# One row block of w3 loaded as float32 through ScalarE's DMA queue and cast on VectorE, in a fused recurrence and feed-forward kernel

## The chip, the cores and the metric

The kernel runs on one core of a Trainium2 chip. The metric is the device time of one execution in microseconds, lower being better. The engines are TensorE (PE; its weight loads are listed as PEld), VectorE (DVE), ScalarE (ACT), GpSimd (POOL) and SyncE (SP). They run side by side and wait for one another by semaphores. Each executes its own instructions strictly in the order in which the program lists them. DMAs are issued from the queues of SP, ACT and POOL.

## The reference

A gated linear recurrence over 768 steps, for 4 batches of 8 heads with 48 channels, gives `x` (3072 tokens by 384). A feed-forward block without a nonlinearity follows; its two elementwise factors are linear in `x`.

```
for t in range(S):
    cur = einsum('bhd,bhe->bhde', u[None] * kt, vt)
    y[:, :, t] = einsum('bhd,bhde->bhe', rt, state + cur)
    state = wt[:, :, :, None] * state + einsum('bhd,bhe->bhde', kt, vt)
a = x @ w1;  b = x @ w2          # 384 -> 1024
h = (a * b) @ w3                 # 1024 -> 1024
return h @ w_out                 # 1024 -> 384
```

Inputs and output are float32.

## The kernel before

**Weights.** Since `(a*b) @ w3 @ w_out = (a*b) @ (w3 @ w_out)`, the kernel first forms `w34 = w3 @ w_out` (1024 by 384). `w3` is kept as `w3_bf`, 8 row blocks of 128 rows by 1024 columns in bfloat16. For a row block `fi`, eight 128x128 pieces are transposed on PE into PSUM in two steps of four (`wt_fi_0` and `wt_fi_1`, columns 0 to 511 and 512 to 1023; L435). They are copied to SBUF in two steps (`w3Te_fi_h`, ACT or DVE, L443). Two steps of four matmuls against `wo_bf` follow (`wm_fi_0`, `wm_fi_1`, L449), and the sum is copied out as a block of `w34` (`w34e_fi`, L454).

**Recurrence.** The 768 positions are cut into 6 chunks of 128, and these into 13 units: the first two hold one batch each, the others two batches. A unit `t` loads `win`, `kin`, `rin`, `vin` (L401), takes a logarithm (`ln_t`, ACT), forms cumulative sums by a matmul against the triangular matrix `LT` (`cs_t`, L510, and for the first three units transposed, `csT_t`, L538), exponentials, products, transposes, masked scores (`m_t`, L671), outputs (`y_t`) and a state update (`kv_t`). In units 8 to 12 the transposes of r and k are DMA transposes on SP's queue (`dtr_t`, `dtk_t`, L593 and L608), and from unit 7 on that of y is too (`dty_t_b`, L733).

**Feed-forward.** A unit's output is multiplied by `w1` and `w2` (`a_t_g`, `b_t_g`, L797), the product is formed (`asb`, `abT`) and multiplied by `w34` (`o_t_b`, L821), copied (`osb`) and stored (`st`).

**Loads.** Everything that changes type on its way (r, k, v and all weights, float32 in memory, bfloat16 in SBUF) is issued by GpSimd, and so are the w tiles but the first. `w3` comes in six pieces: `w3_0` to `w3_3` are two row blocks by 512 columns each (`w3_1`: blocks 2 and 3, first half of the columns; `w3_3`: the same blocks, second half), `w3_4` is blocks 4 and 5 whole, `w3_5` blocks 6 and 7 whole. `w_out` comes in two halves, `wo_0` and `wo_1`. SP carries `win_0`, the row `u`, later the DMA transposes and the stores. Tiles are taken from small sets of buffers, so that a load may wait for an older reader of its buffer; a GpSimd load also waits for the landing of the eighth GpSimd load before it.

**What sets the order.** Two text tables do. `PLACES` says which buffer or PSUM bank each tile takes. `ORDER` lists every step with its engine; the program is emitted in exactly this order. A step named `warmB@N` issues N matmuls of zeros into bank B (L385). They compute nothing that is used, and they need only the `zeros` tile (L295). The constant `LT` is set to ones by DVE (step `ones`, L299) and made triangular by GpSimd (step `LT`, L310); `I128`, the identity for the transposes, is made in the same manner (steps `ones2` and `I128`, L314).

```
    def copier(eng):
        return nc.scalar.copy if eng == "ACT" else nc.vector.tensor_copy

    for n, (f0, f1, g0, g1) in enumerate(W3_PARTS):
        @op(f"w3_{n}")
        def _(eng, f=slice(f0, f1), gs=slice(g0, g1)):
            nc.gpsimd.dma_start(w3_bf[:, f, gs], w3r[:, f, gs])
```

Of the kernel before, what the change touches and what calls it, by code (L numbers as in the profile page):

```python
# [7 lines left out]
F32 = mybir.dt.float32  # L8
# [6 lines left out]
PAIRS = []  # L15
UNITS = [
# [35 lines left out]
W3_PARTS = [(0, 2, 0, 512), (2, 4, 0, 512), (0, 2, 512, 1024), (2, 4, 512, 1024), (4, 6, 0, 1024), (6, 8, 0, 1024)]  # L52
# [44 lines left out]
"""
ORDER = """
win_0@SP table@ACT padr_2@DVE padlw1@DVE ones2@DVE urow@SP w3_1@POOL padkk0@DVE padS1@DVE w3_5@POOL ones@DVE
padlw0@DVE padet0@DVE zeros@DVE win_1@POOL I128@POOL kin_0@POOL w3_3@POOL rin_0@POOL wo_0@POOL wo_1@POOL vin_0@POOL  # L100
warm6@17 wt_7_0@PE wt_7_1@PE w3_2@POOL wt_3_0@PE ln_1@ACT LT@POOL kin_1@POOL ln_0@ACT ucast@ACT rin_1@POOL warm6@8
wt_3_1@PE csT_1@PE w3_0@POOL cs_1@PE wt_2_0@PE rk_0@DVE ne_1@ACT wt_6_0@PE w3_4@POOL w3Te_7_0@DVE csT_0@PE
w3Te_3_0@ACT cs_0@PE padr_0@DVE padkk1@DVE umm@PE wt_6_1@PE wt_2_1@PE ucp@ACT ne_0@ACT ruk_0@DVE trr_0@PE w3Te_7_1@ACT
w3Te_3_1@DVE wm_7_0@PE win_2@POOL KRk_0@DVE w3Te_2_0@ACT padet1@DVE dg_0@DVE trk_0@PE pc_1@ACT wm_3_0@PE et_0@ACT
w3Te_6_0@DVE mask@POOL padS0@DVE trke_0@ACT wm_7_1@PE padr_1@DVE et_1@ACT vin_1@POOL KRr_0@DVE w3Te_6_1@DVE wm_3_1@PE
kin_2@POOL m_0_0@PE w34e_3@ACT wm_2_0@PE mcp_0_0@DVE pc_0@ACT rin_2@POOL wm_6_0@PE dv_0@DVE maff_0_0@DVE trr_1@PE
w1_1@POOL rk_1@DVE y_0@PE w34e_7@DVE yd_0@PE wm_6_1@PE win_3@POOL w3Te_2_1@DVE KRk_1@DVE wt_0_0@PE w34e_6@ACT
wt_1_0@PE yb_0@DVE wt_1_1@PE wm_2_1@PE w3Te_1_0@DVE KRr_1@DVE w3Te_1_1@ACT kv_0@PE padrr1@DVE wt_0_1@PE S_0@DVE
vin_2@POOL trk_1@PE w3Te_0_0@ACT wm_1_0@PE trke_1@DVE w34e_2@ACT ruk_1@DVE m_1_0@PE w3Te_0_1@DVE w1_0@POOL Sb_0@ACT
yt_0@PE mcp_1_0@DVE wm_1_1@PE wm_0_0@PE ln_2@ACT xT_0@DVE maff_1_0@DVE kin_3@POOL wm_0_1@PE dg_1@DVE w34e_1@ACT  # L110
dv_1@DVE cs_2@PE wt_4_0@PE rin_3@POOL padrr0@DVE ne_2@ACT y_1@PE yd_1@PE wt_4_1@PE csT_2@PE yb_1@ACT w3Te_4_0@DVE
wt_5_0@PE w2_0@POOL KRk_2@DVE pc_2@ACT wt_5_1@PE et_2@ACT w3Te_5_0@DVE trk_2@PE w3Te_4_1@DVE trr_2@PE w2_1@POOL
rk_2@DVE trke_2@ACT kv_1@PE KRr_2@DVE w1_3@POOL w3Te_5_1@ACT S_1@DVE warm1@2 m_2_1@PE ruk_2@DVE m_2_0@PE mcp_2_1@ACT
yt_1@PE mcp_2_0@DVE wm_4_0@PE ln_3@ACT wm_4_1@PE win_4@POOL maff_2_1@DVE maff_2_0@DVE wm_5_0@PE w34e_4@ACT dg_2@DVE
w34e_0@ACT y_2@PE w1_2@POOL iw_3@ACT cs_3@PE dv_2@DVE kv_2@PE ne_3@ACT vin_3@POOL a_0_0@PE S_2@DVE xT_1@ACT yd_2@PE
e_3@ACT KRk_3@DVE a_1_0@PE w2_2@POOL asb_0_0@DVE yb_2@ACT wm_5_1@PE pc_3@ACT rw_3@DVE yt_2@PE w34e_5@ACT rin_4@POOL
trk_3@PE asb_1_0@ACT KRr_3@DVE trke_3@ACT xT_2@DVE trr_3@PE w2_3@POOL rk_3@DVE b_2_0@PE trre_3@DVE a_2_0@PE kin_4@POOL
ruk_3@DVE m_3_0@PE asb_2_0@DVE m_3_1@PE win_5@POOL mcp_3_0@ACT a_2_1@PE abT_2_0@DVE b_0_0@PE mcp_3_1@ACT asb_2_1@DVE
b_1_0@PE abT_0_0@DVE Sb_1@ACT maff_3_1@POOL a_2_3@PE dg_3@DVE ln_4@ACT b_2_1@PE win_6@POOL Sb_2@ACT abT_1_0@DVE
# [54 lines left out]
def kernel(  # L174
# [248 lines left out]

    for n, (f0, f1, g0, g1) in enumerate(W3_PARTS):
        @op(f"w3_{n}")
        def _(eng, f=slice(f0, f1), gs=slice(g0, g1)):
            nc.gpsimd.dma_start(w3_bf[:, f, gs], w3r[:, f, gs])  # L427

    def w34_block(fi):
        for h in range(2):  # L430
            @op(f"wt_{fi}_{h}")
# [450 lines left out]
```

## Time and profile before

| | |
|---|---|
| three runs | 165.88, 169.48 and 171.12 us; median 169.48 us |
| the profiled execution | 166.03 us, of which the span from the first to the last instruction is 164.3 us |
| PE busy | 155.3 us, 94% of the span |
| DVE, ACT, POOL busy | 129.0, 111.0 and 77.4 us |
| DMA in GpSimd's queue | 16.06 MB |
| DMA in SP's queue | 8.72 MB |

The profile follows one execution. Its windows view gives the busy time of each engine in chosen stretches, its timeline the instructions in order of time (a row merges neighbours of one kind: start, duration from the first start to the last end, engine, line, operation, tiles, count, and in brackets the idle time before it with what ended it). The chain of waits goes back from the last instruction through whatever released each step. A DMA's time to landing runs from the start of its issue to the arrival of its completion semaphore. The names in rows are those of tiles; all weight tiles read as `w_bf` or `wo_bf`.

### The profile page before, as it was taken

The page shows a single profiled execution, that of the slowest core. Times are in us where ns is not written, and L with a number is a line of the kernel's source. Part 1 is how long each engine was busy: PE and PEld are TensorE (multiplying, and loading weights), DVE is VectorE, ACT ScalarE, POOL GpSimd, SP SyncE. Part 2 cuts the span into 40 slices and gives each one's busy share as a digit, 9 for nine tenths or more (in the row PEclk, how much of TensorE's full clock was granted, in tenths as well). Part 3 has the DMA queues.
Part 4 walks back from the last instruction along what each step waited for, and adds up shares of the span by engine and source line. Part 5 has one row for each costly group of instructions (what it writes and reads, how often), then busy time and mean ns, then how long its engine had stood idle before and what let it go on. Part 6 is the DMA issues. An engine that isn't in the chain of part 4 may idle for free.

```text
span 164.3 us, 4497 instructions
## 1 busy us (share of the span) xinstructions
PE 155.3 (94%) x1852; PEld 118.0 (72%) x1852; DVE 129.0 (79%) x229; ACT 111.0 (68%) x191; POOL 77.4 (47%) x80
## 2 busy tenths in 40 slices
PE   3979999999999999999999999979999999999991
PEld 1336566778897788877797976659779778888760
DVE  4004798999999999999999999969999998535440
ACT  3026637997998989999997889856989341325321
POOL 7956967787798878868379537000000000000000
PEclk9999999999999999999999999999999999999999
DMA  4999999999999999999999999999656230233132
GB/s 73 142 203 195 182 233 172 186 165 227 167 223 151 168 148 186 209 200 159 153 217 204 149 161 129 174 182 190 163 141 97 72 100 0 56 92 141 51 134 107
DMA packets 101606, 25.06 MB, mean 153 GB/s; under 512 B 91777, under 2 KB 99970, under 8 KB 101586
## 3 DMA queue, kind: packets, MB, share of 16 engines
q0 software_dynamic: 81536, 16.06, 116.0%
q1 hardware_dynamic: 20050, 8.72, 26.5%
q8 instruction: 14, 0.23, 0.6%
q14 instruction: 6, 0.05, 0.1%
HBM read 27.79 MB, written 4.72 MB: 198 GB/s over the span
## 4 chain that ended last, share of the span: by engine, by line
PE 78%; DMA 15%; POOL 2%; DVE 2%; issue 1%; ACT 0%; ACTq 0%; POOLq 0%
PE banks L797 38%; PE banks L821 17%; DMA RT<-RR 5%; DMA w_bf<-in_moe_w_dram 5%; DMA rin<-in_r_dram 5%; PE banks L671 4%; PE banks L449 4%; PE banks L709 3%; PE banks L510 2%; PE banks L705 2%; PE banks L759 2%; PE banks L614 2%; PE banks L743 1%; PE banks L599 1%; POOL w_bf L427 1%
## 5 line engine op out<-in xcount | busy, mean ns | idle before, releaser
L797 PE MATMUL banks<-xT,w_bf 128*128 128x256 bf16 (+1 forms) x624 | 69.5, 264 | 0.2 <-DMA xT<-yb 0.2
L797 PEld LDWEIGHTS <-w_bf 128*128 128x128 bf16 x624 | 55.4, 98 | 8.3 <-DMA xT<-yb 0.6
L807 DVE TENSOR_TENSOR abT<-a_sb,banks 128x512 bf16<-128x512 f32 x48 | 32.0, 682 | 9.6 <-PE banks L797 4.7
L803 ACT COPY a_sb<-banks 128x512 f32<-128x512 f32 x43 | 24.8, 589 | 20.9 <-PE banks L797 18.0
L821 PE MATMUL banks<-w,abT 128*128 128x384 bf16 x192 | 34.7, 326 | 0.0
L821 PEld LDWEIGHTS <-abT 128*128 128x128 bf16 x192 | 18.4, 98 | 10.3
L677 ACT CAST Mbf<-banks 128x1024 bf16<-128x1024 f32 x14 | 13.9, 1017 | 7.6 <-PE banks L671 6.7
L401 POOL DMA_DIRECT2D kin<-in_k_dram x13 | 14.6, 1122 | 5.7 <-DVE KK L529 3.6
L494 ACT ACTIVATE lw<-win 128x768 bf16<-128x768 f32 (+1 forms) x13 | 10.3, 799 | 10.0 <-DMA win<-in_w_dram 9.9
L401 POOL DMA_DIRECT2D vin<-in_v_dram x13 | 14.6, 1122 | 3.6 <-DVE RR L335 1.3
L401 POOL DMA_DIRECT2D win<-in_w_dram x12 | 13.9, 1161 | 3.7 <-DMA win<-in_w_dram 1.3
L622 DVE TENSOR_TENSOR rk<-rin,kin 128x768 bf16<-128x768 bf16 (+1 forms) x13 | 6.8, 520 | 11.1 <-DMA rin<-in_r_dram 11.1
L401 POOL DMA_DIRECT2D rin<-in_r_dram x13 | 14.6, 1121 | 1.9 <-DMA vin<-in_v_dram 0.7
L680 DVE TENSOR_TENSOR Mbf<-banks,mask 128x1024 bf16<-128x1024 f32 x10 | 12.1, 1220 | 1.4 <-PE banks L671 1.4
L449 PE MATMUL banks<-wo_bf,w3T 128*128 128x384 bf16 x64 | 12.0, 326 | 0.1
L827 ACT COPY osb<-banks 128x384 f32<-128x384 f32 x20 | 9.7, 486 | 3.3 <-PE banks L821 3.3
L385 PE MATMUL banks<-zeros 128*128 128x512 bf16 x27 | 9.2, 507 | 2.7 <-DVE zeros L295 2.7
L648 DVE TENSOR_REDUCE dg<-ruk 128x16 f32<-128x768 bf16 (+1 forms) x13 | 11.5, 883 | 0.0
L524 ACT ACTIVATE NEt<-banks 128x768 bf16<-128x768 f32 (+1 forms) x13 | 10.1, 775 | 1.8 <-PE banks L510 1.6
L779 ACT CAST Sbf<-Sst 64x384 bf16<-64x384 f32 (+1 forms) x22 | 10.6, 480 | 0.2
L726 DVE TENSOR_TENSOR yb<-banks,dv 128x768 bf16<-128x768 f32 x10 | 9.5, 954 | 0.7 <-issue 0.3
L671 PE MATMUL banks<-RT,KT 64*128 64x128 bf16 x192 | 7.8, 217 | 1.3 <-DMA RT<-RR 1.2
(86 smaller groups left out, 231.7 us busy)
## 6 DMA issues: line engine op xcount, KB each, us to landing
out_dram<-osb SPq DMA_DIRECT2D x24, 192.0 KB, 2.1
win<-in_w_dram POOLq DMA_DIRECT2D x11, 384.0 KB, 9.9
kin<-in_k_dram POOLq DMA_DIRECT2D x11, 192.0 KB, 10.3
rin<-in_r_dram POOLq DMA_DIRECT2D x11, 192.0 KB, 9.5
vin<-in_v_dram POOLq DMA_DIRECT2D x11, 192.0 KB, 10.0
w_bf<-in_moe_w_dram POOLq DMA_DIRECT2D x8, 192.0 KB, 9.3
w_bf<-in_moe_w_dram POOLq DMA_DIRECT2D x4, 256.0 KB, 8.4
w_bf<-in_moe_w_dram POOLq DMA_DIRECT2D x2, 512.0 KB, 9.4
```

The lines of the kernel that those rows point to most:

```text
L401: QUEUE[eng].dma_start(dst, src)
L449: nc.tensor.matmul(one(f"wm{fi}")[:, :DM], lhsT=x[:, gi, :], rhs=wo_bf[:, gi, :], start=(gi == 0), stop=(gi == FI - 1))
L494: nc.scalar.activation(LW[:, :, :D], ww, Act.Ln)
L648: nc.vector.reduce_sum(dgs, ruks, axis=AX.X)
L671: nc.tensor.matmul(o[:, e, q, :], lhsT=KTs[a:a + PAD, b * HP + q, :], rhs=RTs[a:a + PAD, b * HP + q, :], start=True, stop=True)
L677: nc.scalar.copy(Mbf[m], mview())
L680: nc.vector.tensor_mul(Mbf[m].rearrange("s j q t -> s (j q) t"), mview().rearrange("s j q t -> s (j q) t"), mask[:, None, :].to_broadcast( ...
L779: copier(eng)(Bp[e * PAD:(e + 1) * PAD, :, e, :], Sp[e * PAD:(e + 1) * PAD])
L797: nc.tensor.matmul(o[:, f, :], lhsT=wt[:, di, fi * P:(fi + 1) * P], rhs=x[:, di, :T], start=(di == 0), stop=(di == DI - 1))
L803: copier(eng)(sa, one(f"a{t}_{g}"))
L807: nc.vector.tensor_mul(ab[:, g * per:(g + 1) * per, :T], sa.rearrange("p (f t) -> p f t", t=T), one(f"b{t}_{g}").rearrange("p (f t) -> p f ...
L821: nc.tensor.matmul(one(f"o{t}_{b}{x_}")[:, :c1 - c0], lhsT=ab[:, fi, off + b * C:off + (b + 1) * C], rhs=w34[:, fi, c0:c1], start=(fi == 0 ...
```

## The change

`w3_5` is cut to row block 6 alone. Row block 7 is loaded as float32 into a new tile `w3f` (128 by 1024) by step `w3h`, which stands first in `ORDER` and is issued by ACT, and step `w3c` on DVE casts it into `w3_bf`. Both tables are replaced from end to end. The steps are otherwise the same, with other buffers, banks and places. The zero matmuls are 17, 10, 3 and 2 in place of 17, 8 and 2.

```
+W3_HW = 7
-W3_PARTS = [(0, 2, 0, 512), (2, 4, 0, 512), (0, 2, 512, 1024), (2, 4, 512, 1024), (4, 6, 0, 1024), (6, 8, 0, 1024)]
+W3_PARTS = [(0, 2, 0, 512), (2, 4, 0, 512), (0, 2, 512, 1024), (2, 4, 512, 1024), (4, 6, 0, 1024), (6, 7, 0, 1024)]
...
+    if W3_HW is not None:
+        w3f = sb.tile([P, DFF], F32, name="w3f")
+
+        @op("w3h")
+        def _(eng):
+            QUEUE[eng].dma_start(w3f, w3r[:, W3_HW, :])
+
+        @op("w3c")
+        def _(eng):
+            copier(eng)(w3_bf[:, W3_HW, :], w3f)
```

Two lines of the new `ORDER`, the first and the third:

```
+w3h@ACT win_0@SP padrr0@DVE padr_0@DVE urow@SP table@ACT win_1@POOL padrr1@DVE padr_1@DVE padkk1@DVE ones2@DVE
...
+kin_0@POOL ucast@DVE ln_0@ACT w3_3@POOL wo_0@POOL wo_1@POOL ln_1@ACT w3_0@POOL warm7@17 wt_3_0@PE rin_1@POOL umm@PE
```

Up to the first `wm` step PE runs, before: 17 zero matmuls, `wt_7_0 wt_7_1 wt_3_0`, 8 zero matmuls, `wt_3_1 csT_1 cs_1 wt_2_0 wt_6_0 csT_0 cs_0 umm wt_6_1 wt_2_1 trr_0 wm_7_0`. Now: 17 zero matmuls, `wt_3_0 umm wt_7_0 wt_7_1 cs_1 csT_0`, 10 zero matmuls, `wt_3_1 csT_1 cs_0 wt_6_0 wt_6_1 wt_2_0`, 3 zero matmuls, `wm_3_0`. Lines of the new kernel are 1 higher than before up to the loads and 12 higher after them.

GpSimd's first rows, before (the two loads ahead are `w3_1` and `w3_5`; after the identity come `kin_0`, `w3_3`, `rin_0`, `wo_0` with `wo_1`, `vin_0`, `w3_2`, and then the triangle `LT`):

```order
L427 DMA w_bf<-in_moe_w_dram 128x2x512
L427 DMA w_bf<-in_moe_w_dram 128x2x1024
L401 DMA win_78<-in_w_dram 128x8x48
L314 ISA
L314 AFFINE_SELECT I_153<-I_153 128x128
L401 DMA kin_69<-in_k_dram 128x8x48
L427 DMA w_bf<-in_moe_w_dram 128x2x512
L401 DMA rin_64<-in_r_dram 128x8x48
L422 DMA wo_bf<-in_moe_w_out_dram 128x4x384 x2
L401 DMA vin_72<-in_v_dram 128x8x48
L427 DMA w_bf<-in_moe_w_dram 128x2x512
L310 AFFINE_SELECT LT<-LT 128x128
```

The same stretch of GpSimd now (`win_1`, `w3_1`, the halved `w3_5`, `rin_0`, the identity, `LT`, then `kin_0`, `w3_3`, `wo_0` with `wo_1`, `w3_0`):

```order
L402 DMA win_79<-in_w_dram 128x8x48
L428 DMA w_bf<-in_moe_w_dram 128x2x512
L428 DMA w_bf<-in_moe_w_dram 128x1024
L402 DMA rin_62<-in_r_dram 128x8x48
L315 ISA
L315 AFFINE_SELECT I_153<-I_153 128x128
L311 AFFINE_SELECT LT<-LT 128x128
L402 DMA kin_67<-in_k_dram 128x8x48
L428 DMA w_bf<-in_moe_w_dram 128x2x512
L423 DMA wo_bf<-in_moe_w_out_dram 128x4x384 x2
L428 DMA w_bf<-in_moe_w_dram 128x2x512
```

`LT` has moved ahead of `kin_0`, `w3_3` and both halves of `w_out`.

DVE's rows from the memset ahead of `LT`'s ones to the first product, before:

```order
L340 MEMSET Sbf_128 128x384
L299 MEMSET LT 128x128
L300 MEMSET ones_c 128x1
L320 MEMSET lw_82 128x16x8
L345 MEMSET ETt_92 128x8x2
L295 MEMSET zeros 128x256
L622 TENSOR_TENSOR rk_109<-rin_64,kin_69 128x384
```

And now, from the same ones to the cast of `u`:

```order
L307 MEMSET ones_r 1x128
L296 MEMSET zeros 128x256
L439 CAST w_bf<-w3f 128x1024
L331 MEMSET KK_95 128x16x8
L300 MEMSET LT 128x128
L301 MEMSET ones_c 128x1
L321 MEMSET lw_82 128x16x8
L321 MEMSET lw_83 128x16x8
L358 CAST u_one<-u_row 1x384
```

The cast of the new tile stands ahead of the memset of `LT`, and `zeros` ahead of both, with eight memsets before it in place of eleven.

More of the change, by code (lines that the diff above doesn't have):

```diff
@@ L97 @@
+dv12=1 m12_0=5,6 M12_0=3 m12_1=0,1 M12_1=2 y12=5,6 yb12=0 xT12=2 a12_0=0 b12_0=4 sa12_0=1 abT12=2 a12_1=7 b12_1=2
+sa12_1=2 a12_2=6 b12_2=1 sa12_2=0 a12_3=5 b12_3=4 sa12_3=1 o12_0=2 so12_0=3 o12_1=3 so12_1=2
 """
 ORDER = """
[L99 to L101 removed]
@@ L102 @@
[L102 to L116, printed above, removed]
```

192 lines of the change are left out of this document (103 added, 89 removed).

## The prediction

> **What bounds the kernel now.** The page comes first, for who is busy.
>
> ```profile
> span 164.3 us, 4497 instructions
> PE 155.3 (94%) x1852; PEld 118.0 (72%) x1852; DVE 129.0 (79%) x229; ACT 111.0 (68%) x191; POOL 77.4 (47%) x80
> ...
> L385 PE MATMUL banks<-zeros 128*128 128x512 bf16 x27 | 9.2, 507 | 2.7 <-DVE zeros L295 2.7
> ```
>
> PE is idle for only 9.0 us, and 9.2 us of its busy time are zero matmuls. An edit that leaves the real matmuls alone can win only from these. The windows view says where the idle time lies (columns: stretch, its length, then busy time and count by engine, granted clock, DMA share, GB/s).
>
> ```profile
> 0.00:12.00 12.00, 8.18 (x33) 3.37 (x34) 1.75 (x12) 2.16 (x4) 9.03 (x17) 1.00 1.03 138
> 12.00:36.00 24.00, 23.60 (x289) 15.56 (x287) 19.27 (x45) 16.68 (x34) 18.37 (x21) 1.00 1.84 189
> 36.00:100.00 64.00, 64.00 (x897) 52.76 (x896) 61.82 (x100) 58.41 (x99) 48.48 (x43) 1.00 2.12 182
> 100.00:112.00 12.00, 10.59 (x131) 7.84 (x129) 10.21 (x19) 9.43 (x16) 1.57 (x2) 1.00 1.73 156
> 112.00:160.00 48.00, 48.00 (x507) 38.17 (x506) 35.96 (x56) 23.76 (x42) 0.00 (x0) 1.00 0.43 101
> 160.00:164.30 4.30, 0.88 (x6) 0.30 (x4) 0.00 (x0) 0.58 (x2) 0.00 (x0) 1.00 0.33 119
> ```
>
> Idle: 3.8 us in the first 12, 0.4 up to 36, nothing to 100, 1.4 up to 112, nothing to 160, and 3.4 us of last copy and store. The edit acts on the first stretch. PE's timeline there, and then the two waits of the fourth stretch:
>
> ```profile
> 2.74 6.70 PE L385 MATMUL banks<-zeros 128*128 128x512 bf16 x17 [2.74 <-DVE zeros L295]
> 10.53 0.84 PE L435 MATMUL banks<-I,w_bf 128*128 128x128 bf16 x12 [1.08 <-DMA w_bf<-in_moe_w_dram]
> 11.21 1.89 PE L385 MATMUL banks<-zeros 128*128 128x512 bf16 x8
> 13.04 0.40 PE L435 MATMUL banks<-I,w_bf 128*128 128x128 bf16 x4
> 13.28 0.39 PE L538 MATMUL banks<-LT,lw 128*128 128x128 bf16 x4
> 13.50 0.33 PE L510 MATMUL banks<-lw,LT 128*128 128x384 bf16 x1
> ...
> 14.59 0.33 PE L361 MATMUL banks<-u_one,ones_r 1*128 1x384 bf16 x1
> ...
> 15.88 0.81 PE L449 MATMUL banks<-wo_bf,w3T 128*128 128x384 bf16 x4
> ...
> 103.11 0.82 PE L797 MATMUL banks<-xT,w_bf 128*128 128x256 bf16 x6 [0.21 <-DMA xT<-yb]
> ...
> 108.09 0.62 PE L671 MATMUL banks<-RT,KT 64*128 64x128 bf16 x16 [1.20 <-DMA RT<-RR]
> ```
>
> The first real matmul (`wt_7_0`) waits until 10.53 for `w3_5`; 8 zero matmuls then fill the time to `w3_3` (`wt_3_1`, 13.04), and the first `wm` follows at 15.88. From there PE hardly stops. What each load takes:
>
> ```profile
> 0.81 0.45 SPq L401 DMA_DIRECT2D win<-in_w_dram  x1
> ...
> 1.33 1.57 POOL L427 DMA_DIRECT2D w_bf<-in_moe_w_dram  x2 [0.81 <-POOLq L866]
> 2.88 0.91 POOL L401 DMA_DIRECT2D win<-in_w_dram  x1
> ...
> 4.13 0.91 POOL L401 DMA_DIRECT2D kin<-in_k_dram  x1
> 5.03 0.71 POOL L427 DMA_DIRECT2D w_bf<-in_moe_w_dram  x1
> ...
> 6.61 1.51 POOL L422 DMA_DIRECT2D wo_bf<-in_moe_w_out_dram  x2
> ```
>
> ```profile
> w_bf<-in_moe_w_dram POOLq DMA_DIRECT2D x1, 256.0 KB, 6.5
> win<-in_w_dram SPq DMA_DIRECT2D x1, 192.0 KB, 2.7
> ```
>
> ```profile
> 2.17 8.32 DMA w_bf<-in_moe_w_dram
> ...
> 99.48 8.48 DMA RT<-RR
> ```
>
> ```profile
> DMA to landing us min/median/max: 8.0/8.0/8.0
> ```
>
> ```profile
> DMA to landing us min/median/max: 9.0/9.6/10.2
> ```
>
> The issues stand in the timelines of SP and POOL, the two sizes with landing times (us) in the DMA view of the first 2.1 us, the chain of waits has `w3_5` and a late transpose, and the last two rows are the tile views of `w3_3` alone and of `wo_0` and `wo_1`. So GpSimd's `w3_1` lands at 1.33 + 6.5 = 7.8, `w3_5` at 2.17 + 8.3 = 10.5, `w3_3` at 5.03 + 8.0 = 13.0, just when PE takes it, and `wo_0` at 6.61 + 9.0 = 15.6, 0.3 us ahead of the first `wm`. SP's `win_0` needs 2.7 us.
>
> **The change part by part.** All against the profiled execution: 166.03 us, 164.3 of span and 1.7 around it.
>
> *Start of PE.* `zeros` now has eight short memsets ahead of it. These rows are DVE's, before:
>
> ```profile
> 2.07 0.17 DVE L299 MEMSET LT<- 128x128 bf16 x1
> ...
> 2.42 0.27 DVE L295 MEMSET zeros<- 128x256 f32 x1
> ...
> 14.08 0.42 DVE L443 COPY w3T<-banks 128x512 bf16<-128x512 bf16 x1
> ...
> 21.45 0.55 DVE L454 CAST w<-banks 128x384 bf16<-128x384 f32 x1
> ```
>
> The eighth instruction started at 2.07; the ninth now can about then, so `zeros` and PE start 0.4 us earlier, and the 17 zero matmuls end near 9.0. Gain 0.4.
>
> *First real matmul.* It is now `wt_3_0`, on `w3_1`, which stands second in GpSimd's queue and shares the DMA engines with the new load. Bounds for its landing: 7.8 (as first in the queue) to 10.5 (`w3_5`, second in the queue, twice as large). I take 9.6, between: it is the second, but with half the bytes. PE idles 0.5 in place of 1.08. Gain 0.6, bounds +1.1 to -0.4.
>
> *The new load and cast.* No float32 weight load on ACT's queue is in the trace. Nearest are `win_0` on SP (192 KB in 2.7 us) and `w3_5` on GpSimd (512 KB in 8.3). How busy the DMA engines are meanwhile:
>
> ```profile
> 2.00:3.00 1.00, 0.26 (x1) 0.13 (x2) 0.69 (x6) 0.09 (x1) 1.00 (x3) 1.00 1.03 194
> 3.00:6.50 3.50, 3.50 (x9) 1.21 (x8) 0.00 (x0) 0.00 (x0) 3.42 (x5) 1.00 0.90 97
> 6.50:10.50 4.00, 2.95 (x9) 0.95 (x7) 0.00 (x0) 0.00 (x0) 2.51 (x4) 1.00 1.37 214
> ```
>
> `win_0` moved at 194 GB/s between 2 and 3 us; after it the rate was 97 until 6.5, so there is room. `win_0` and the new tile, 704 KB or 0.72 MB, at 194 GB/s take 3.7 us from 2.0: landing near 5.7. I take that, as SP's row is of the same kind of issue; the far bound is an issue at 0.8 plus 8.3, or 9.1. The cast: 0.84 us if it goes like the copy of 512 columns in 0.42, 1.47 if like the cast of 384 in 0.55. I take 1.2, so it ends at 6.9. PE needs the block only after `wt_3_0`, at 9.6: hidden for 2.7 us. ACT issues for about SP's 0.45 and is else idle then. On DVE the copies and products queued behind the cast all wait for later loads; only the ones for `LT` are urgent.
>
> *What stands behind the cast.* GpSimd reaches `LT` after four loads (1.33 + 0.84 + 0.7 + 2 x 0.91) and the identity, at about 5.0, and waits there for DVE's ones until 7.1. `LT` itself took about 0.3, so `kin_0` is issued at 7.4, `w3_3` at 8.3 (before: 5.03) and `wo_0` at 9.0 (before: 6.61). By their own times to landing `w3_3` would come at 16.3 and `wo_0` at 18.0. By GpSimd's queue as a stream, with 192 + 256 + 256 + 96 + 96 + 256 KB up to `w3_3` against 256 + 512 + 192 + 96 + 256 before, it would come at about 12. What speaks for the stream: 214 GB/s flowed before 10.5 with several loads in flight, and at 7.4 most of 800 KB is still due. Against it: the shortest time to landing of a weight piece was 6.5, which gives 14.8. I take 14.0. PE comes to `wt_3_1` at 9.6 + 1.2 (twelve transposes 0.7, three short steps about 0.2 each from the starts above) + 10 x 0.24 = 13.2. Wait: 0.8, bounds 0 to 3.1.
>
> *Zero matmuls.* 8 took 1.89, 0.24 each. The new order has 5 more in the stretch: cost 1.2. Against this, at `wt_3_1` PE has `umm`, `cs_1` and `csT_0` behind it, which before came later: 0.6 us of work by the starts above. `wt_3_1` starts at 14.0 against 13.04, less 0.6; that is 0.4 later, and the 3 extra zero matmuls add 0.7 if nothing waits beneath them. So at the end of the early stretch PE is 1.1 us late. The earlier start and the smaller hole are within this: what they gain ends in the wait for `w3_3`.
>
> *Late stage.* The waits of 0.21 and 1.20 are for `dty_7` and `dtr_9`. Now `b_6_1` and `b_6_2` (two steps of six matmuls, like the 0.82 row) stand behind `y_7` and give its transpose 1.3 us more. But `kin_9` and `rin_11`, which feed `KRk_9` and `rk_11`, stand later in GpSimd's queue. I take 0.5 off, bounds 1.4 off and 1.5 on.
>
> Sum: 164.3 + 1.1 - 0.5 = 164.9 of span, 166.6 us. That is 2.9 below the median shown, 169.48, and 0.7 above the fastest run, 165.88.
>
> **The rivals.**
>
> *Room in the loads.* In the trace `w3_3` and `wo_0` came within 0.3 us of their use, so any slower DMA falls on PE at once. Of three runs two took 3.5 and 5 us more than the profiled one. If that is such waiting, an order whose first w and r loads stand earlier escapes it: no hole at 9.0 (-1.1), start -0.4, late waits gone (-1.4), zero matmuls +1.2, so 162.6 of span, 164.3 us, 3% below the median. Against: no longer run is traced, and nothing shows where it lost time.
>
> *GpSimd held by the new load* (the slow side). If the new tile lands at 9.1, the cast ends at 10.6 by its upper bound, `LT` at 11.1, `w3_3` is issued at 12.0 and lands 6.5 to 8.0 later: 18.5 to 20.0 against 13.04. Less 0.6 done ahead, PE is 4.9 to 6.4 us late, up to 7.1 with the three zero matmuls; with the late 0.5 off that is 170.4 to 172.6 us, and 171 as its value, near the shorter landing, since the queue would be empty. A loss of 2% (3.3 us) begins where `w3_3` lands at 16.3, so already with my landing of 5.7 if the full 8.0 apply. For it: of the weights that PE takes first, all but `w3_1` and `w3_5` now pass behind `LT`. Against it: the stream.
>
> *One queue of engines.* The new load takes from `w3_1` what it frees in `w3_5`: the first real matmul stays at 10.5, PE comes to `wt_3_1` at 14.1, and `w3_3`, behind the same bytes, 0.5 us later than I set it, at 14.5. That 0.5 goes straight into the sum: 167.1. [...] The 97 GB/s between 3.0 and 6.5 us speak against it here, since unused rate is there to take.
>
> **How the numbers follow.** Forecast 0.35 (166.6; its own range 165.0 to 168.5), room in the loads 0.29 (164.3), GpSimd held 0.27 (171), one queue 0.09 (167.1). The range of 164.0 to 171.2 takes in all but the far end of the third and some of the first's scatter. About 2% is what a measurement of this kernel can tell from no change. The forecast and the one queue lie within it of the profiled execution: 0.44. The room counts as faster, since the longer runs of before are what it escapes: 0.29. GpSimd held counts as slower: 0.27.
>
> **What would show it.** Right: `w3c` starts near 5.7 on DVE, GpSimd is idle before `LT` for about 2 us, `wt_3_1` begins near 14, the row of 10 zero matmuls is followed by a wait under 1.5 us, and PE's idle time from 100 to 112 is about 0.9. Wrong: a landing of `w3f` beyond 7 us; a wait above 3 us at `wt_3_1` or at the first `wm`; or a new wait of PE between 36 and 100, where I found none and assume none. Runs near 170 in spite of an early stretch as forecast would mean that the longer runs come from something that the order of loads doesn't touch.

## The result and the profile after

The new kernel takes 171.62 us (median of 5 runs, 170.77 to 171.81) where the kernel before takes 168.05 (median of 5 on the same chip, 165.88 to 171.12). The ratio is 1.0295, 95% interval 1.0217 to 1.0373: slower, 0.4 us above the range given. Ratios here leave out executions far above the fastest of their kernel; the medians hold all. The profiled execution takes 170.77 us, 4.7 more than before's.

The page and the windows of the new kernel (the last stretch ends with its span):

```profile
span 168.7 us, 4513 instructions
PE 154.9 (92%) x1855; PEld 118.5 (70%) x1857; DVE 130.0 (77%) x231; ACT 112.2 (67%) x191; POOL 76.5 (45%) x79
```

```profile
0.00:12.00 12.00, 7.96 (x41) 3.62 (x42) 3.54 (x19) 3.31 (x5) 10.50 (x19) 1.00 1.10 166
12.00:36.00 24.00, 21.94 (x250) 14.71 (x249) 17.73 (x40) 14.12 (x28) 17.08 (x19) 1.00 1.81 187
36.00:100.00 64.00, 63.90 (x929) 53.12 (x927) 60.09 (x96) 60.88 (x102) 47.58 (x42) 1.00 2.09 181
100.00:112.00 12.00, 10.07 (x121) 7.01 (x120) 8.53 (x15) 9.30 (x16) 1.32 (x2) 1.00 1.55 115
112.00:160.00 48.00, 46.15 (x498) 37.24 (x496) 39.10 (x62) 23.20 (x39) 0.00 (x0) 1.00 0.47 98
160.00:168.70 8.70, 4.87 (x30) 2.74 (x28) 1.02 (x2) 1.43 (x3) 0.00 (x0) 1.00 0.38 137
```

PE does as much as before and idles more: 6.1 us up to 36 (before 4.2, with 0.6 us more of zero matmuls), 3.8 from 100 to 160 (before 1.4). Where the schedule falls back shows in two places of PE's timeline, `cs_4` near 45 us and the last ten matmuls; first before, then after, with the waits:

```profile
44.88 0.48 PE L510 MATMUL banks<-lw,LT 128*128 128x384 bf16 x2
...
159.09 1.79 PE L821 MATMUL banks<-w,abT 128*128 128x384 bf16 x10
```

```profile
2.31 5.30 PE L386 MATMUL banks<-zeros 128*128 128x512 bf16 x17 [2.31 <-DVE zeros L296]
9.34 0.40 PE L447 MATMUL banks<-I,w_bf 128*128 128x128 bf16 x4 [1.73 <-DMA w_bf<-in_moe_w_dram]
...
10.77 2.32 PE L386 MATMUL banks<-zeros 128*128 128x512 bf16 x10
14.08 0.40 PE L447 MATMUL banks<-I,w_bf 128*128 128x128 bf16 x4 [0.98 <-DMA w_bf<-in_moe_w_dram]
...
45.97 0.49 PE L522 MATMUL banks<-lw,LT 128*128 128x384 bf16 x2
...
103.69 1.46 PE L833 MATMUL banks<-w,abT 128*128 128x384 bf16 x8 [1.92 <-DVE Mbf L692]
...
125.25 1.47 PE L809 MATMUL banks<-xT,w_bf 128*128 128x256 bf16 x12 [0.88 <-ACT osb L839]
...
163.08 1.79 PE L833 MATMUL banks<-w,abT 128*128 128x384 bf16 x10
```

At `cs_4` the new kernel is 45.97 - 44.88 = 1.1 us late, at the end 163.08 - 159.09 = 4.0. So 1.1 us are lost early, 2.9 late, and 0.4 behind the last matmul: the 4.4 of the span. This is one pair of executions. In the ten traced executions with the new kernel's early order (the new kernel, e1 to e3, e5, e6, e9, e11, e13, e18) `cs_4` starts between 44.55 and 46.69, in the three with before's (before, e10, e17) between 44.66 and 45.27, so the early share is uncertain by about 1 us. The chain of waits names the first late wait:

```profile
86.05 1.15 POOL win L402
87.20 14.72 DMA kin<-in_k_dram
...
102.42 1.23 DVE Mbf L692
...
103.69 1.47 PE banks L833 x8
```

GpSimd issues `kin_9` behind `kin_10`, `vin_11` and `win_12`, and it lands 14.7 us after its issue. VectorE stands 3.02 us at `KRk_9`; behind it `mcp_8_0` empties the bank that `o_5_1` wants. Next `rk_11` waits for `rin_11`, with `yb_8` and all of unit 8's output behind it:

```profile
4.19 0.88 DVE L439 CAST w_bf<-w3f 128x1024 bf16<-128x1024 f32 x1 [1.95 <-DMA w3f<-in_moe_w_dram]
...
101.94 0.56 DVE L541 TENSOR_TENSOR KK<-kin,NEt 128x768 bf16<-128x768 bf16 x1 [3.02 <-DMA kin<-in_k_dram]
...
108.44 0.56 DVE L634 TENSOR_TENSOR rk<-rin,kin 128x768 bf16<-128x768 bf16 x1 [1.53 <-DMA rin<-in_r_dram]
```

The last figure of a row of the DMA view is the time from issue to landing: after, for `w3f` and `win_0` early, `kin_9` and `rin_11` late; then before's `kin_9` and `rin_11`.

```profile
w3f<-in_moe_w_dram ACTq DMA_DIRECT2D x1, 512.0 KB, 3.4
...
win<-in_w_dram SPq DMA_DIRECT2D x1, 192.0 KB, 4.2
...
kin<-in_k_dram POOLq DMA_DIRECT2D x1, 192.0 KB, 14.7
...
rin<-in_r_dram POOLq DMA_DIRECT2D x1, 192.0 KB, 13.4
```

```profile
kin<-in_k_dram POOLq DMA_DIRECT2D x1, 192.0 KB, 10.7
...
rin<-in_r_dram POOLq DMA_DIRECT2D x1, 192.0 KB, 11.2
```

### The profile page after: what moved, and what is told of

The parts are those of the page before. It is cut to its first block, busy times and chain, and to the rows that moved or that the text cites. A ratio compares the mean times of both kernels' runs of the same rounds, so it can differ in the third digit from the quotient of the medians.

```text
span 168.7 us, 4513 instructions
## 1 busy us (share of the span) xinstructions
PE 154.9 (92%) x1855; PEld 118.5 (70%) x1857; DVE 130.0 (77%) x231; ACT 112.2 (67%) x191; POOL 76.5 (45%) x79
## 4 chain that ended last, share of the span: by engine, by line
PE 57%; DMA 24%; DVE 6%; ACT 5%; issue 2%; POOL 2%; SPq 1%; DVEq 0%; ACTq 0%
PE banks L809 26%; PE banks L833 14%; DMA kin<-in_k_dram 9%; DMA win<-in_w_dram 7%; DMA wo_bf<-in_moe_w_out_dram 5%; PE banks L721 2%; PE banks L461 2%; DMA w3f<-in_moe_w_dram 2%; PE banks L522 2%; PE banks L683 2%; PE banks L626 2%; PE banks L717 1%; PE banks L611 1%; DMA out_dram<-osb 1%; PE banks L771 1%
## 5 line engine op out<-in xcount | busy, mean ns | idle before, releaser
L809 PE MATMUL banks<-xT,w_bf 128*128 128x256 bf16 (+1 forms) x624 | 68.7, 264 | 0.9 <-ACT osb L839 0.9
L815 ACT COPY a_sb<-banks 128x512 f32<-128x512 f32 x44 | 25.5, 590 | 14.4 <-PE banks L809 13.3
L402 POOL DMA_DIRECT2D rin<-in_r_dram x13 | 14.7, 1130 | 3.7 <-DVE rk L634 3.0
L506 ACT ACTIVATE lw<-win 128x768 bf16<-128x768 f32 (+1 forms) x13 | 10.4, 803 | 5.0 <-DMA win<-in_w_dram 4.9
L455 DVE COPY w3T<-banks 128x512 bf16<-128x512 bf16 x14 | 5.5, 414 | 9.0 <-ACT w3T L455 5.3
L386 PE MATMUL banks<-zeros 128*128 128x512 bf16 x30 | 8.6, 437 | 2.4 <-DVE zeros L296 2.3
L541 DVE TENSOR_TENSOR KK<-kin,NEt 128x768 bf16<-128x768 bf16 (+1 forms) x13 | 6.8, 520 | 4.6 <-DMA kin<-in_k_dram 4.6
```

Of the source, the lines that this page charges most:

```text
L402: QUEUE[eng].dma_start(dst, src)
L506: nc.scalar.activation(LW[:, :, :D], ww, Act.Ln)
L809: nc.tensor.matmul(o[:, f, :], lhsT=wt[:, di, fi * P:(fi + 1) * P], rhs=x[:, di, :T], start=(di == 0), stop=(di == DI - 1))
L815: copier(eng)(sa, one(f"a{t}_{g}"))
```

## The experiments

Each kernel ran beside the kernel before on its chip, and ratios are to that. A trace shows one execution of each. Diffs of GpSimd's order show its steps from `win_10` on. In both kernels nine loads follow `win_10`, from 80 to 101 us. Two theories run through the texts on record: by A, the loss is the new places of `kin_9` and `rin_11`; by B, the DMA engines have more to move in that stage than they can, and some transfer or other comes late.

### One or two loads moved: e1, e2, e3

```
-win_10 vin_10 kin_10 vin_11 win_12 kin_9 vin_9 dv_7 rin_12 dv_8 rin_11 maff_8_1 vin_12
+win_10 vin_10 kin_9 kin_10 vin_11 win_12 vin_9 dv_7 rin_12 dv_8 rin_11 maff_8_1 vin_12        (e1)
+win_10 vin_10 kin_10 vin_11 win_12 kin_9 vin_9 rin_11 dv_7 rin_12 dv_8 maff_8_1 vin_12        (e2)
+win_10 vin_10 kin_9 kin_10 vin_11 win_12 vin_9 rin_11 dv_7 rin_12 dv_8 maff_8_1 vin_12        (e3)
```

> The changed kernel with one load moved: kin_9 ahead of kin_10, vin_11 and win_12 in GpSimd's queue. Theory A (the late order of GpSimd's loads makes the loss): DVE's 3.0 us wait of KRk_9 for kin_9 goes, and with it PE's 1.9 us wait at o_5_1; but DVE then comes to rk_11 earlier and waits about 4 us for rin_11 in place of 1.5, so that part of it is given back at y_9 and a_8: 1 to 2 us off, span 167 to 168. Theory B (the DMA engines are overloaded from 90 to 110 us, whichever load goes first): another load becomes as late, less than 0.7 us off. Theory C (the loss is all in the early stretch): no change.

> The changed kernel with one load moved: rin_11 ahead of dv_7, rin_12 and dv_8 on GpSimd, kin_9 left late. Theory A: the wait of KRk_9 stays at 3 us and o_5_1's 1.9 us on PE with it; the 1.5 us wait of rk_11 goes, yb_8 comes 1.5 us earlier, and the waits at y_9 and at a_8_3 shrink: 1 to 1.5 us off. Theory B: less than 0.7 us off. Theory C: no change.

> Both loads moved. Theory A: neither wait is left, PE's idle time from 100 to 130 us falls from 3.9 to under 1 us, 2.5 to 3.5 us off the changed kernel, span 165.2 to 166.2, within 1% of the kernel before. Theory B: a wait for another load or a DMA transpose of over 2 us takes their place, less than 1 us off. Theory C: no change.

Measured: e1 1.0349 (1.0250 to 1.0447), e2 1.0232 (1.0158 to 1.0305), e3 1.0232 (1.0156 to 1.0309). In each the wait aimed at is gone, and another stands in its place. VectorE's and PE's longest late waits in e1:

```profile
109.45 0.56 DVE L634 TENSOR_TENSOR rk<-rin,kin 128x768 bf16<-128x768 bf16 x1 [5.85 <-DMA rin<-in_r_dram]
```

```profile
109.58 0.40 PE L683 MATMUL banks<-RT,KT 64*128 64x128 bf16 x8 [2.35 <-DMA KT<-KK]
```

VectorE's in e2, then PE's in e3:

```profile
104.48 0.56 DVE L541 TENSOR_TENSOR KK<-kin,NEt 128x768 bf16<-128x768 bf16 x1 [4.39 <-DMA kin<-in_k_dram]
```

```profile
111.15 1.04 PE L683 MATMUL banks<-RT,KT 64*128 64x128 bf16 x16 [3.43 <-DMA KT<-KK]
```

With `kin_9` early `rin_11` is later, with `rin_11` early `kin_9` is, and with both early the DMA transpose `dtk_9` takes 10.4 us to land. That the two places alone make the loss is refuted. Behind the 3.43 us PE also runs at a lower clock for a while, as the windows of e3 show (granted clock: third figure from the end):

```profile
108.00:110.00 2.00, 0.00 (x0) 0.00 (x0) 1.90 (x4) 0.00 (x0) 0.00 (x0) 0.96 2.15 160
...
112.00:114.00 2.00, 2.00 (x10) 0.87 (x7) 0.93 (x2) 1.73 (x2) 0.00 (x0) 0.50 0.39 81
114.00:116.00 2.00, 2.00 (x10) 1.24 (x9) 0.45 (x1) 1.06 (x2) 0.00 (x0) 0.50 1.13 192
116.00:118.00 2.00, 2.00 (x26) 1.69 (x25) 1.75 (x3) 0.35 (x2) 0.00 (x0) 0.83 0.76 145
```

### The load without the order, the order without the load: e4, e7

```
 e4 = the kernel before, with
+W3_HW = 7;  (6, 8, 0, 1024) -> (6, 7, 0, 1024);  w3h@ACT first in ORDER;  w3c@DVE behind zeros@DVE
 e7 = the new kernel, with
-W3_HW = 7;  (6, 7, 0, 1024) -> (6, 8, 0, 1024);  without w3h and w3c
```

> The kernel before in its own order and places, with the new load alone: w3h first on ACT, w3c on DVE behind zeros, w3_5 halved. The new tile lands near 4.2 us, as in the changed kernel, so wt_7 starts when the 17 zero matmuls end, and the later loads come about 1 us earlier for the half of w3_5 that left GpSimd's queue. If the load itself is good: the 1.1 us hole goes and w3_3 lands near 12.2, 0.5 to 1.5 us off the kernel before. If the load only takes from the others (one queue of engines): the hole goes, w3_3 lands at 13 as before, and less than 0.5 us comes off.

> The new order without the new load: w3_5 brings row blocks 6 and 7 again, and the float32 load and its cast are gone. This is the fourth corner beside before, the load in the old order (0.995) and the new kernel (1.0295). If the load is worth as much in the new order as in the old (0.5%) or more, the ratio is 1.033 to 1.045: wt_7_0 then waits for w3_5 near 11 us, and w3_3, with 256 KB more ahead of it, lands near 15 in place of 14.0. If the load hurts in the new order (its bytes delay what stands behind it), the ratio is below 1.028.

Measured: e4 0.9951 (0.9909 to 0.9992), e7 1.0360 (1.0305 to 1.0416). In the old order the load gains 0.5% (0.9951). In the new order its share is not told apart: the intervals around 1.0295 and 1.0360 overlap, and e7's execution has `cs_4` at 45.16, 0.8 us ahead of the new kernel's. The new order costs some 3.5% with the load (1.0295 / 0.9951 = 1.0346) and without it (1.0360). Of the two halves of the change the load does no harm, and the order makes the whole loss.

### Unit 9 and the stores put back: e5, e9, and one store moved in the kernel before: e10

```
 e5 = the new kernel, with
+win_10 kin_10 vin_9 kin_9 vin_10 rin_11 vin_11 dv_7 win_12 dv_8 maff_8_1 rin_12 vin_12
+DVE: abT_6_2 KRk_9 KRr_9 abT_5_0;  SP: dtk_9 dtr_9
 e9 = e5, with
+SP: st_2_0 st_3_0 dtk_8 st_1_0 st_3_1 dtr_8 dty_7_1 dty_7_0 dtk_9 dtr_9 st_4_0;  osb_6_0, st_6_0 behind mcp_9_1
 e10 = the kernel before, with
+SP: dtr_8 st_4_0 dty_7_0 dty_7_1 dtk_9 dtr_9 dty_8_1
```

> The new kernel with the whole supply of unit 9 put back as it stood before, on three engines: GpSimd's last loads in the old sequence (kin_10, vin_9, kin_9, vin_10, rin_11, vin_11, dv_7, win_12, dv_8, maff_8_1, rin_12, vin_12), KRk_9 ahead of KRr_9 and of abT_5_0 on VectorE, and dtk_9 ahead of dtr_9 on SP. Early order, load, banks and the rest stay new. Theory A2 (the loss is the order in which unit 9 is supplied, through all three queues, not only the two loads moved so far): dtk_9 is issued near 99 us and landed near 105, m_9 waits at most 1.5 us, PE's clock stays 1.00, span 165.3 to 166.6, ratio to before 1.004 to 1.012 (the early 1.0 us stays). Theory B (the DMA engines carry more than they can between 83 and 110 us in the new schedule, whichever load goes first): another landing is late by 2 us or more, PE waits for it, span 168 or more, ratio 1.02 or more.

> The kernel with the supply of unit 9 put back (e5), and SP's stores put back as well: st_3_0 ahead of dtk_8 and st_4_0 behind dtr_9, where the old order has them (in the new one both stand at 89 to 90 us, ahead of dty_7, dtk_9 and dtr_9; osb_6_0 and st_6_0 move back with them, since they reuse its buffer). Theory S (these two stores, 384 KB, stand in the stream ahead of unit 9's transposes and delay them): dty_7 lands near 102.5 in place of 104.2 and 104.5, dtk_9 and dtr_9 by 108.5 in place of 110.6, m_9's wait falls from 2.38 us to 1.2 or less and a_7_1's from 1.29 to 0.3 or less, span 165.2 to 166.2, ratio 1.003 to 1.013. Rival: the stores don't matter, landings within 0.7 us of e5's, span 167 or more, ratio 1.018 or more.

> The kernel before, with one step moved: st_4_0 ahead of dty_7_0 on SP, as the new order has it, in place of behind dty_8_1. Theory S: one more store of 192 KB in the stream ahead of unit 9's transposes makes dty_7 and dtr_9 land 1.0 to 1.5 us later (dtr_9 near 109.2 in place of 107.96), PE's wait at m_9 grows from 1.20 to 2.2 to 2.7 us, and the ratio is 1.005 to 1.012, or 1.02 where the wait passes 3 us and the clock falls. Rival: no change, ratio 0.997 to 1.003.

Measured: e5 1.0267 (1.0149 to 1.0386), e9 1.0150 (1.0027 to 1.0273). So the old late order on GpSimd, with unit 9's on VectorE and SP, doesn't heal it either; PE in e5 waits for unit 7's transpose and then for unit 9's:

```profile
104.56 0.83 PE L809 MATMUL banks<-xT,w_bf 128*128 128x256 bf16 x6 [1.29 <-DMA xT<-yb]
...
110.74 0.62 PE L683 MATMUL banks<-RT,KT 64*128 64x128 bf16 x16 [2.38 <-DMA RT<-RR]
```

In e9's execution (170.13 us; its runs lie between 167.40 and 171.14) unit 7's came 2.7 to 4.0 us earlier, as the theory of the stores asked, but `dtr_9` landed at 110.1, near e5's 110.6, and m_9 waited 3.89: the theory failed where it counted. e10 has no interval (its 4 runs lie between 166.06 and 170.34, median 169.62, beside 166.69). In its profile, of the run of 170.34, PE waits 2.06 us for unit 7's transpose and 2.59 at m_9, the second as forecast; the clock falls without a wait past 3 us (0.66 from 110 to 112 us, 0.50 to 114). How much of this is the store's is not told apart, since before's own long executions beside it reach 169.41 and none of these is traced:

```profile
104.75 0.82 PE L797 MATMUL banks<-xT,w_bf 128*128 128x256 bf16 x6 [2.06 <-DMA xT<-yb]
...
111.13 1.04 PE L671 MATMUL banks<-RT,KT 64*128 64x128 bf16 x16 [2.59 <-DMA RT<-RR]
```

### Zero matmuls in the stall: e6

```
 e3 with
+warm3@12 m_9_0@PE
```

> The kernel with both loads moved (e3), with 12 more zero matmuls ahead of m_9_0, where PE stood idle for 3.43 us; they need nothing that is late and compute nothing that is used. Theory C (an idle time of over 3 us is paid twice, since the granted clock then falls to 0.5 for about 6 us): the idle time ahead of m_9 falls below 0.8 us, the granted clock between 110 and 118 us is 1.00 in place of 0.50 to 0.83, and the span falls from 170.3 by the 3 us or so that the half clock costs, to 166.5 to 167.8; ratio to before 1.00 to 1.012. Rival D (the clock falls for another reason, such as what PE or the DMA engines did before, or the late chain through VectorE and the transposes sets the end anyway): clock or end as in e3, span 169.5 to 170.5, ratio 1.02 to 1.03.

Measured: 1.0205 (1.0128 to 1.0281), e3's 1.0232 within the interval. The clock stayed at 1.00 from 104 to 120, as theory C said (its "over 3 us" is the author's estimate from e3's one wait of 3.43 us; e10's clock fell within 2.59 us of idle time, e18's stayed at 1.00 through 3.21), but the end did not move: PE was 1.7 us ahead of e3 at 96 us, and `dtk_9` still landed at 110.6 (e3: 111.1), with new waits of 1.10 and 1.56 us for `a_sb` and `vin_9` on the way. In this execution the stream of transfers set the pace, not PE. `rin_11`, in the same place of the same order as in e3, took 23.3 us to land, and VectorE waited 6.36 us for it (e3: 0.35); so one order of loads can give very different landings. The price of the clock alone stays undetermined.

### Transfers taken out of the crowd: e11, e13

```
 e11 = the new kernel, with
+win_10 kin_10 kin_9 vin_9 dv_7 dv_8 rin_11 maff_8_1 win_12 rin_12 vin_10 vin_11 vin_12
 e13 = the new kernel, with
-vin_10 vin_11 win_12 vin_12      (left out; vin_11's buffer is that of vin_8)
```

> The new kernel with three loads taken out of the crowd: win_12, vin_10 and vin_11 (384 KB each in memory), and rin_12 and vin_12 with them, are issued behind maff_8_1, near 100 us, in place of 80 to 92; they are needed at 115, 121 and 132. Theory B (between 83 and 110 us the DMA engines have more than they can move, and whichever transfer stands last in that crowd is late): kin_9 lands before 97 in place of 101.9, rin_11 before 103 in place of 108.4, dtk_9 and dtr_9 before 107, the waits of KRk_9, o_5_1, rk_11 and m_9 together fall below 1.5 us, span 165 to 166.3, ratio 1.00 to 1.012. Theory A (only the places of kin_9 and rin_11 among the loads count): kin_9 is better by its two places, but rin_11 stays behind dv_8 and late, span above 167. If a third thing sets the pace (SP's issue, VectorE's order), landings come earlier and the span stays at 168 to 169.

> The new kernel without four of GpSimd's last nine loads: win_12, vin_10, vin_11 and vin_12 are left out (units 10 to 12 compute with what lies in their buffers), and every other step keeps its place. It leaves out 1.5 MB of transfers and no work of PE, VectorE or ScalarE. Theory B (the late loss is DMA work between 83 and 118 us, whichever step it falls on): kin_9 lands before 97, dtk_9 before 105, PE idles less than 0.5 us in all between 100 and 160 us (3.8 us in the new kernel), span 164.8 to 165.6, which is the old span and the early 1.0 us; ratio 0.997 to 1.007. Rival (the order of the steps on PE, VectorE and SP makes the late waits): idle time from 100 to 160 stays above 1.5 us, span above 166.5, ratio above 1.01.

Measured: e11 1.0167 (1.0094 to 1.0239), e13 0.9993 (0.9952 to 1.0034). In e11 `kin_9` lands at 94.3, `rin_11` at 101.7, `dtk_9` at 107.4; PE doesn't idle from 100 to 112. But the loads put off to 101 to 107 us now stand among the transposes of units 8, 10 and 11, and 2.7 us of PE's waits appear there, behind a store that took 5.4 us to land and for whose buffer ScalarE waited 3.59; PE's longest:

```profile
119.96 0.62 PE L683 MATMUL banks<-RT,KT 64*128 64x128 bf16 x16 [1.53 <-ACT a_sb L815]
```

e13 decides between the order of the steps and the transfers. It leaves every step of PE, VectorE, ScalarE and SP in its place, and its windows have no idle time from 100 to 136, where the new kernel has 3.8 us:

```profile
100.00:112.00 12.00, 12.00 (x160) 9.17 (x159) 11.91 (x23) 11.01 (x20) 0.15 (x1) 1.00 0.84 132
112.00:136.00 24.00, 24.00 (x281) 19.24 (x279) 23.11 (x37) 16.20 (x27) 0.00 (x0) 1.00 0.59 109
```

Its span is 163.8 us, less than forecast, since before's own 1.4 us of late idle time went too. So the late loss needs the DMA work between 83 and 118 us, on whichever step it falls; with four loads fewer, the new order of the steps leaves PE no idle time there. The kernel before without these loads was not run. Why the same nine loads cost 1.4 us of late idle time in the old order and 3.8 in the new one is not shown by this: from 80 to 104 us the DMA engines moved 4.22 MB before and 4.24 MB now.

### The early stretch: e8, e16

```
 e8 = e4, with       +win_1 I128 w3_3 wo_0 kin_0 rin_0 wo_1
 e16 = the new kernel, with  +w3_5 w3_3 rin_0 I128 LT wo_0 kin_0 wo_1
```

> The old order with the load (e4), and w3_3 and wo_0 moved ahead of kin_0 and rin_0 in GpSimd's queue. In e4 PE's one early wait is 1.03 us at wt_3_1, for w3_3. If that wait sets the early lateness, w3_3 lands 0.5 to 0.9 us earlier, the schedule from 20 to 100 us is 0.4 to 0.9 us ahead of e4, and the span is 163.0 to 163.4, ratio to before 0.989 to 0.994. If the next late thing (kin_0 and rin_0 for trr_0, or w_out's halves) takes its place, the ratio is 0.995 to 1.002.

> The new kernel with the early part of the mending alone: w3_3 right behind w3_5, wo_0 right behind LT. If PE's early 1.0 us is the wait for w3_3 behind LT, w3_3 lands near 12, the wait at wt_3_1 (0.98 us) goes, and the schedule from 46 to 98 us is 0.5 to 0.9 us ahead of the new kernel. Theory B: this doesn't come through, since the stream of DMAs sets the late stage; PE idles more after 100 us and the ratio stays at 1.022 to 1.03. If late steps simply follow PE, the gain comes through whole: ratio 1.021 to 1.026.

Measured: e8 1.0042 (0.9991 to 1.0093), e16 1.0342 (1.0253 to 1.0431). In e8 the wait for `w3_3` goes and one of 1.56 us at `trr_0` comes, for `rin_0`. In e16 `w3_3` lands at 11.1, and `cs_4` runs at 44.45, 1.5 us earlier than in the new kernel; in e14, with the same early order, at 44.57. So the early lateness goes with that wait, though e6 got to 44.55 without this edit. None of it reaches the end: `kin_9` still lands at 101.6, PE waits longer, and the clock falls (a mean of 0.72 from 100 to 112 us).

```profile
103.34 2.72 PE L833 MATMUL banks<-w,abT 128*128 128x384 bf16 x8 [3.09 <-DVE Mbf L692]
```

```profile
100.00:112.00 12.00, 8.91 (x80) 5.77 (x80) 8.66 (x15) 6.63 (x12) 0.00 (x0) 0.72 1.37 110
```

### Mended versions: e12, e14, e15, e17, e18

```
 e12 = e4, with               +win_10 kin_10 vin_9 kin_9 rin_11 dv_7 win_12 dv_8 maff_8_1 rin_12 vin_10 vin_11 vin_12
 e15 = e4, e17 = before, with +win_10 kin_10 vin_9 kin_9 vin_10 rin_11 dv_7 win_12 dv_8 maff_8_1 rin_12 vin_11 vin_12
+vin11: the buffer of vin_8, so issued behind y_8;  vin12: the buffer of vin_9, behind y_9
 e14 = the new kernel, early as e16, late as
+win_10 vin_10 kin_10 kin_9 vin_9 rin_11 dv_7 win_12 dv_8 maff_8_1 rin_12 vin_11 vin_12   (vin_11, vin_12 as e15; VectorE and SP as e5)
 e18 = the new kernel, with
+win_10 vin_10 kin_10 win_12 kin_9 vin_9 dv_7 rin_12 dv_8 rin_11 maff_8_1 vin_11 vin_12   (vin_11, vin_12 as e15)
```

> The old order with the load (e4), and vin_10 and vin_11 issued behind rin_12, near 101 us, in place of 85 to 88; they are needed at 117 and 127. Theory B: rin_11, win_12, dty_7, dtk_9 and dtr_9 land 1.5 to 3 us earlier than in e4, PE's waits of 0.31 and 1.03 us at a_7_1 and m_9 go, span 162.0 to 163.0, ratio to before 0.980 to 0.990. If these waits are not of the DMA's making, the ratio stays at 0.995.

> The new kernel mended at both ends: w3_3 right behind w3_5 and wo_0 right behind LT in GpSimd's queue (early); kin_9, vin_9 and rin_11 ahead of dv_7, win_12 behind it, rin_12 behind maff_8_1, vin_11 and vin_12 behind y_8 and y_9 in the buffers of vin_8 and vin_9, KRk_9 and KRr_9 ahead of abT_5_0 and dtk_9 ahead of dtr_9 (late). Theory B with the early stretch as read: the schedule from 46 to 98 us is 0.5 to 0.9 us ahead of the new kernel, dtk_9 and dtr_9 land by 107, PE's idle time from 100 to 136 us is below 1.2 us, span 164.3 to 165.5, ratio 0.995 to 1.006. If the crowd only moves once more: idle time above 2.5 us there, ratio 1.015 or more.

> The old order with the load (e4), and only vin_11 and vin_12 moved: behind y_8 and y_9, in the buffers of vin_8 and vin_9, so that they can't be issued before about 100 and 113 us; they are needed at 127 and 137. One load less stands ahead of unit 9's transposes, and none more ahead of dty_8, which was late in e12. Theory B: dtk_9 and dtr_9 land 1 to 2 us earlier than in e4, PE's waits at a_7_1, m_9 and a_8_1 together fall below 0.5 us, span 162.4 to 163.2, ratio 0.983 to 0.992. Rival: what is gained at m_9 is lost at dty_8 again, ratio 0.995 to 1.01.

> The kernel before, with the two late v loads of e15 alone (vin_11 behind y_8 in vin_8's buffer, vin_12 behind y_9 in vin_9's) and without the float32 load: what part of e15's gain (0.9929) is the load's. If the early load is worth its 0.5% on top, the ratio is 0.996 to 1.000. If the relief late is all of it, 0.990 to 0.995. In both, no execution near 169 to 170, which the kernel before has, since PE then has no late stall after which the clock falls.

> The new kernel with the same two late v loads and nothing else. Theory B: one load less stands ahead of kin_9 and two less ahead of dtk_9, dty_8 and dtk_11, so kin_9 lands near 99 to 100 in place of 101.9 and dtk_9 near 107; half to all of the late 3 us goes, ratio 1.003 to 1.017. If the places of kin_9 (behind kin_10 and win_12) and rin_11 (behind dv_8) are what counts, KRk_9 and rk_11 still wait by 1.5 us or more each, ratio 1.02 to 1.03.

Measured: e12 1.0104 (1.0057 to 1.0151): unit 9's transposes land 2 us earlier than in e4 and both waits go, but the put-off loads now stand ahead of `dty_8`, which takes 6.5 us to land, and `a_8_1` waits 2.11. e15 0.9929 (0.9898 to 0.9960), 164.29 us, is 0.7% faster than before and so beats both kernels. Its two loads are held back by their buffers and issued at 102.7 and 112.1, behind unit 9's transposes, which land at 101.6 and 106.1 (before: loads at 88.7 and 100.4, transposes at 103.9 and 108.0). PE has no idle time from 84 to 136.

```profile
100.00:112.00 12.00, 12.00 (x160) 9.27 (x159) 11.75 (x23) 11.03 (x20) 2.06 (x2) 1.00 1.33 170
```

e17, the same without the new load: 0.9953 (0.9920 to 0.9986), 164.49 us. The intervals overlap, so the load's share in e15 is not told apart. Both shrink the spread: 12 runs of e17 lie between 164.09 and 164.89, while 17 of the kernel before beside them lie between 164.24 and 168.74. Since e17 changes only the two late v loads, before's longer executions come from this stage.

On the new order the relief fails. e14 spreads from 165.55 to 172.26 (median 169.36, no interval): PE ran 1.4 us ahead at 95 us, then waited 1.56 and 3.15 us for transposes. e18 is the worst of all, 1.0506 (1.0273 to 1.0739), above both ratios on record. With one load less in the crowd, `kin_9` landed at 106.2 in place of 101.9, and others were late too. The DMA view of e18 for `vin_10`, and `win_12` and `dtr_8`; the same of the new kernel for `vin_10` and `dtr_8`:

```profile
vin<-in_v_dram POOLq DMA_DIRECT2D x1, 192.0 KB, 18.8
...
win<-in_w_dram POOLq DMA_DIRECT2D x1, 384.0 KB, 18.2
RT<-RR SPq DMA_TRANSPOSE x1, 14.9
```

```profile
vin<-in_v_dram POOLq DMA_DIRECT2D x1, 192.0 KB, 9.4
...
RT<-RR SPq DMA_TRANSPOSE x1, 8.6
```

`vin_10` was issued 0.2 us earlier than in the new kernel and landed 9 us later, though nothing ahead of it in GpSimd's queue had changed. In the eight other executions with the same loads ahead of it, it took 9.2 to 14.3 us, so the loads ahead don't set a landing alone; whether e18's 18.8 comes of what stands behind it is not shown. From 84 to 100 us e18 moved 140 GB/s, the new kernel 183. So the amount of work is not all. The rate at which it is done differs too, and why it fell here stays open.

## Why the prediction was wrong

The forecast was 166.6 us, within 2%; the direction was right for the early stretch and wrong for the late one.

- *Start of PE.* As forecast: the zero matmuls begin 0.4 us earlier (2.31 against 2.74) and end earlier than 9.0, at 7.6, since 17 took 5.3 us in place of 6.7.
- *First real matmul.* Forecast 9.6, measured 9.34. The rival of the one queue, 10.5, falls. PE idles 1.73 us ahead of it, but what it gains ends in the wait for `w3_3`, as said.
- *The new load and cast.* Cheaper than taken: landing at 0.80 + 3.37 = 4.17 in place of 5.7, the cast 0.88 us in place of 1.2. `win_0` paid some of it, 4.2 us in place of 2.7, but there was rate to spare: from 2.0 to 4.2 us the DMA engines moved 307 GB/s, where before they moved 139.
- *What stands behind the cast.* GpSimd waited 0.21 us for `LT`, not 2. `wt_3_1` began at 14.08 after 0.98 us of wait; forecast 14.0 and 0.8. This hit is luck: `w3_3` was issued at 6.56, 1.7 us ahead of the 8.3 in the sum, and took 7.5 us to land where 14.0 left it 5.7, and the two errors cancel. "GpSimd held by the new load" gave 171 us, near the result, by a mechanism that did not occur.
- *Zero matmuls.* The early sum said 1.1 us late; `cs_4` is 1.1 late. The sum rests on `w3_3`'s landing, and the executions scatter by 2 us here, so the match is in part luck too.
- *Late stage.* This is the step that failed: "I take 0.5 off, bounds 1.4 off and 1.5 on". It is 2.9 on, and 0.4 more behind the last matmul. The places of `kin_9` and `rin_11` were seen, but the bound of 1.5 for them had no working behind it, and the waits for `dty_7` and `dtr_9` were taken as a matter of PE's order. In their stead PE waited 1.92 us behind `kin_9`, which took 14.7 us to land (before 10.7), and in all 3.8 us from 100 to 160, where the sum left 0.9 of before's 1.4. e1 to e3 and e5 show that putting those places right moves the wait instead of ending it, and e13 that it ends when four loads go. What was missing was a look at the DMA engines in that stage: the row of 36 to 100 us in the prediction has a DMA share above 2 and 182 GB/s, second only to the 189 from 12 to 36, and it was read for PE alone. It would have warned that a place in a queue need not bound a landing there (`vin_10`, with the same loads ahead of it, took 9.2 to 18.8 us over the executions), but not said which order loses, since both kernels move much the same there (4.22 and 4.24 MB from 80 to 104 us). Why the new order falls worse stays open.
- *Room in the loads.* Its premise, that before's longer executions come from the early loads, is refuted by e17.

## What to carry to other kernels

From 36 to 100 us, where the DMA engines moved 182 GB/s before and 181 now, a load's price was not its place in its own queue: e1 to e3 moved two loads ahead, and the waits moved on to others of 2.35 to 5.85 us. In such a stage add up all loads, stores and transposes that are in flight, ask which are needed late, and hold just these back (in e15 a buffer whose last reader comes late did it, with issues at 102.7 and 112.1 us) until those that are needed soon have landed. Then measure it: this helped in the old order (e15, e17) and not in the new (e14, e18). Judge a change of load and a change of order apart, since here one won 0.5% in the old order and the other lost 3.5%. A wait that vanishes is a result only when the end moves with it.

## What the runs showed of the hardware

- In several runs the granted clock fell while PE was idle and stayed low behind the idle time: in e3 it fell to 0.50 when PE had been idle for 2.1 us of its 3.43, in e16 after 2.2 of 3.09, in e10 after 2.1 of 2.59 (worked out from the mean clock in windows of 2 us). It stayed there for 6.8, 6.8 and 3.4 us, past the end of the idle time. It did not fall in 3.21 us of idle time in e18 or 3.17 in e7, so these runs show no length of idle time that decides it.
- The same GpSimd load of 192 KB, `rin_11`, took 5.9 us to land in e11 and 23.3 in e6. In e18 `dtk_8`, issued 3.4 us behind `vin_10`, landed 4.1 us ahead of it.
- A float32 load of 512 KB by ScalarE's queue at the very start landed in 3.4 us. In the kernel before, GpSimd's first load, `w3_1`, which casts 512 KB in memory to 256 KB in SBUF, landed in 6.5, and `w3_5`, twice that, in 8.3.
